# A second transfer on ScalarE's DMA queue: x's half-units 8 to 46 of a scaled addition

## The chip, the cores and the metric

The kernel runs on one core of a Trainium2 chip. A core has five engines with an instruction stream each (TensorE, VectorE or DVE, ScalarE or ACT, GpSimd or POOL, and the sync engine or SP) and 16 DMA engines that move bytes between HBM, the chip's main memory, and SBUF, the core's own memory of 128 partitions. An instruction on SP or ACT issues a transfer; the transfer's share for each DMA engine is then queued there. Engines are tied together by semaphores: a finished instruction or a landed transfer raises one, and others wait for it.

The metric is the device time of one execution in microseconds (us), as the median of several runs.

## The reference

```python
B, S, D = 512, 32, 640
x, fx: (512, 32, 640) bf16, normal * 0.05;  alpha: (1,) bf16
def reference(x, fx, alpha):
    return x + alpha * fx
```

Each of the three large tensors (x, fx and the result) has 10,485,760 elements of two bytes, 20.97 MB. The kernel so reads 41.94 MB, writes 20.97 MB, and does one multiplication and one addition for each element.

## The kernel before

Each large tensor is viewed as 128 rows of 81,920 elements, one row for each partition. A row is cut into 160 half-units of 512 elements, which are 1 KB for each partition and 128 KB for all of them. The whole of x lies in SBUF in one tile, `x_t`, which also takes the result. fx goes through two buffers of 23 half-units (`f_t`, a pool with `bufs=2`).

Four lists say how the work is cut. `X` (line 17) has six loads of x, of 8, 38, 46, 23, 39 and 6 half-units; `F` (line 18) has seven loads of fx, six of 23 half-units and one of 22; `S` (line 19) has three stores, of 64, 64 and 32 half-units. A step of computing, `c j`, belongs to `f j`: on DVE, a `tensor_scalar` (line 96) multiplies the buffer by alpha in place, and a `tensor_tensor` (line 99) adds it to the same columns of `x_t`, in place. So `c 0` works on half-units 0 to 23 and needs x 0, x 1, f 0 and alpha; `c 1` works on 23 to 46 and needs x 1 and f 1; `c 2` needs x 2 and f 2.

The order of all work is the list `PLAN` (lines 22 to 47), written out by hand; nothing is reordered. Its first steps are x 0, x 1, a, f 0, f 1, x 2, c 0, f 2, c 1, f 3, x 3, c 2. The step `a` loads alpha, two bytes, and spreads it to 128 partitions with a `matmul` (line 113) against a row of ones and a copy on DVE (line 115).

Every transfer goes through `transfer` (lines 77 to 82), which issues it on SP. SP works in order. At the start it issues six transfers without waiting: x 0, x 1, alpha, f 0, f 1 and x 2. The transfer f 2 has to wait until `c 0` has read its buffer, f 3 until `c 1` has, and so on. `LATE` (line 48) holds the first store back until f 6 has landed. A last instruction on SP (line 123) waits for everything but the last store.

Of the kernel before, what the change touches and what calls it, by code (L numbers as in the profile page):

```python
# [1 line left out]

# [4 lines left out]

ACT = mybir.ActivationFunctionType
ALU = mybir.AluOpType
F32 = mybir.dt.float32  # L10
BF16 = mybir.dt.bfloat16

K = 512
P = 128


X = [(0, 8), (8, 46), (46, 92), (92, 115), (115, 154), (154, 160)]
F = [(0, 23), (23, 46), (46, 69), (69, 92), (92, 115), (115, 138), (138, 160)]
S = [(0, 64), (64, 128), (128, 160)]
N = 160  # L20

PLAN = """
x 0
x 1
a
f 0
f 1
x 2
c 0
f 2  # L30
c 1
f 3
x 3
c 2
f 4
x 4
c 3
f 5
c 4
f 6  # L40
x 5
c 5
c 6
s 0
s 1
s 2
"""
LATE = {("s", 0): ("f", 6)}


@with_exitstack
def kernel(
    ctx: ExitStack,
    tc: tile.TileContext,
    x: bass.AP,
    fx: bass.AP,
    alpha: bass.AP,
    out: bass.AP,
):
    nc = tc.nc  # L60
    xv = x.flatten_outer_dims().rearrange("(p n) d -> p (n d)", p=P)
    fxv = fx.flatten_outer_dims().rearrange("(p n) d -> p (n d)", p=P)
    ov = out.flatten_outer_dims().rearrange("(p n) d -> p (n d)", p=P)
    assert xv.shape[1] == N * K

    consts = ctx.enter_context(tc.tile_pool(name="consts", bufs=1))
    psum = ctx.enter_context(tc.tile_pool(name="psum", bufs=1, space=bass.MemoryType.PSUM))
    whole = ctx.enter_context(tc.tile_pool(name="whole", bufs=1))
    fs = ctx.enter_context(tc.tile_pool(name="fs", bufs=2))
    ctx.enter_context(tc.manual_schedule())  # L70

    sync = mybir.DependencyInfo(mybir.DependencyClass.Sync, mybir.DependencyReason.DATA)
    xt = whole.tile([P, N * K], x.dtype, name="x_t")
    ft, moved = {}, {}
    done = []

    def transfer(what, out, in_):
        r = nc.sync.dma_start(out=out, in_=in_)  # L78
        if what in LATE:
            tc.add_manual_dep(r.ins, moved[LATE[what]].ins.name, sync, reason="issue late")  # L80
        moved[what] = r
        done.append(r)

    def load_x(i):
        a, b = X[i]
        transfer(("x", i), xt[:, a * K : b * K], xv[:, a * K : b * K])

    def load_f(j):
        a, b = F[j]
        ft[j] = fs.tile([P, max(e - s for s, e in F) * K], fx.dtype, tag="f", name="f_t")  # L90
        transfer(("f", j), ft[j][:, : (b - a) * K], fxv[:, a * K : b * K])

    def compute(j):
        a, b = F[j]
        term, total = ft[j][:, : (b - a) * K], xt[:, a * K : b * K]
        nc.vector.tensor_scalar(  # L96
            out=term, in0=term, scalar1=lanes["a_f"][:], scalar2=None, op0=ALU.mult
        )
        done.append(nc.vector.tensor_tensor(out=total, in0=total, in1=term, op=ALU.add))  # L99

    def store(i):
        a, b = S[i]
        transfer(("s", i), ov[:, a * K : b * K], xt[:, a * K : b * K])

    lanes = {}

    def alpha_to_lanes():
        a_1 = consts.tile([1, 1], alpha.dtype, name="a_1")
        transfer("a", a_1[:], alpha[None, :])
        ones = consts.tile([1, P], alpha.dtype, name="ones")  # L110
        nc.vector.memset(ones[:], 1.0)  # L111
        a_ps = psum.tile([P, 1], F32, name="a_ps")
        done.append(nc.tensor.matmul(a_ps[:], ones[:], a_1[:], start=True, stop=True))  # L113
        lanes["a_f"] = consts.tile([P, 1], F32, name="a_f")
        nc.vector.tensor_copy(out=lanes["a_f"][:], in_=a_ps[:])  # L115

    does = {"x": load_x, "f": load_f, "c": compute, "s": store, "a": alpha_to_lanes}
    for step in PLAN.split("\n"):
        if step:
            what, *of = step.split()  # L120
            does[what](*map(int, of))

    rest = nc.sync.nop(nofuse=True)
    for i in done[:-1]:
        tc.add_manual_dep(rest.ins, i.ins.name, sync, reason="all but the last store")


# [1 line left out]
_INS = ['x', 'fx', 'alpha']  # L129
_OUTS = [((512, 32, 640), 'bfloat16')]  # L130


# [23 lines left out]
```

## Time and profile before

The median of three runs is 151.09 us (151.01 to 151.16). The profile shows one further execution, which took 151.26 us. Its span, from the first instruction to the last, is 149.5 us.

| | |
|---|---|
| profiled execution | 151.26 us |
| its span | 149.5 us |
| DVE busy | 66.7 us, 45% of the span |
| PE and POOL busy | 0.2 us each |
| ScalarE busy | no row in the profile |
| bytes moved by DMA | 62.92 MB, 421 GB/s over the span |
| DMA queue | one, q1, whose packets took 98.2% of the 16 engines' span |
| issue of a transfer on SP | 0.33 to 0.64 us |

In the profile L78 is line 78 of the kernel, "SPq" is SP's sequencer at work on issuing, and "a<-b" says that a is written from b. The time "to landing" of a transfer runs from the start of its issue to its last arrival. A packet is one descriptor's worth of bytes; here each packet is one partition's share of a transfer, so a transfer on 128 partitions has 128 packets of data, eight on each DMA engine. In a table of stretches, a packet is counted in the stretch in which it starts, so that a short stretch can show a DMA share above 1.

### The profile page before, as it was taken

Reading aid. Unit: us, or ns where it says so; the run is one execution under the profiler, and the core shown is the slowest. Engines: PE = TensorE matmul, PEld = TensorE weight load, DVE = VectorE, ACT = ScalarE, POOL = GpSimd, SP = SyncE. Lnnn points to the kernel's source line nnn. Section 1 sums busy time; section 2 is a strip of 40 time slices with the busy share of each in tenths; the row PEclk is TensorE's granted clock in tenths of the full one; section 3 lists DMA queues with packets and bytes.
Section 4 is the critical chain, followed back from the end, with each engine's and each line's share of the span. In section 5 each row is a group of like instructions: output and inputs, shape, how many; then the busy total and the mean of one; then the engine's idle time right before and its main releaser. Section 6 shows DMA issues by size and latency. Waiting matters only on the chain.

```text
span 149.5 us, 93 instructions
## 1 busy us (share of the span) xinstructions
PE 0.2 (0%) x1; PEld 0.1 (0%) x1; DVE 66.7 (45%) x16; POOL 0.2 (0%) x4
## 2 busy tenths in 40 slices
PE   0000000000000000000000000000000000000000
PEld 0000000000000000000000000000000000000000
DVE  0000005999950099999499104999960000000000
POOL 0000000000000000000000000000000000000000
DMA  5998999999979999999998999999996969696994
GB/s 151 463 500 354 448 410 466 435 403 466 542 303 410 466 435 403 429 460 422 443 502 353 417 460 390 458 515 438 403 561 281 561 281 561 281 561 281 456 456 210
DMA packets 2306, 62.92 MB, mean 421 GB/s; under 512 B 258, under 2 KB 258, under 8 KB 386
## 3 DMA queue, kind: packets, MB, share of 16 engines
q1 hardware_dynamic: 2306, 62.92, 98.2%
HBM read 41.94 MB, written 20.97 MB: 421 GB/s over the span
## 4 chain that ended last, share of the span: by engine, by line
DMA 41%; DVE 31%; issue 1%; SPq 1%; DVEq 0%
DMA f_t<-in_fx_dram 41%; DVE x_t L99 20%; DVE f_t L96 11%; SPq L78 1%; DVEq L96 0%
## 5 line engine op out<-in xcount | busy, mean ns | idle before, releaser
L99 DVE TENSOR_TENSOR x_t<-x_t,f_t 128x11776 bf16<-128x11776 bf16 (+1 forms) x7 | 43.8, 6254 | 0.2
L96 DVE TENSOR_SCALAR f_t<-f_t,a_f 128x11776 bf16<-128x11776 bf16 (+1 forms) x7 | 22.9, 3265 | 26.7 <-DMA f_t<-in_fx_dram 26.7
L115 DVE COPY a_f<-a_ps 128x1 f32<-128x1 f32 x1 | 0.2, 159 | 16.2 <-PE a_ps L113 16.2
L111 DVE MEMSET ones<- 1x128 bf16 x1 | 0.2, 165 | 0.8 <-PEq L140 0.8
L113 PE MATMUL a_ps<-a,ones 1*128 1x1 bf16 x1 | 0.2, 158 | 17.0 <-DMA a<-in_alpha_dram 17.0
L140 POOL MEMSET const-bfloat16-1.0<- 128x1 bf16 x1 | 0.1, 101 | 0.0
L140 POOL MEMSET const-uint8-127<- 128x1 uint8 x1 | 0.1, 101 | 0.0
L113 PEld LDWEIGHTS <-ones 1*128 1x128 bf16 x1 | 0.1, 98 | 1.0 <-DVE ones L111 1.0
L140 POOL MEMSET const-float32-0.0<- 128x1 f32 x1 | 0.1, 98 | 0.2 <-issue 0.2
L140 POOL MEMSET const-float32-1.0<- 128x1 f32 x1 | 0.1, 98 | 0.0
## 6 DMA issues: line engine op xcount, KB each, us to landing
f_t<-in_fx_dram SPq DMA_DIRECT2D x6, 2944.0 KB, 19.4
x_t<-in_x_dram SPq DMA_DIRECT2D x1, 5888.0 KB, 41.9
x_t<-in_x_dram SPq DMA_DIRECT2D x1, 4992.0 KB
x_t<-in_x_dram SPq DMA_DIRECT2D x1, 4864.0 KB, 15.9
out_dram<-x_t SPq DMA_DIRECT2D x1, 4096.0 KB, 38.1
x_t<-in_x_dram SPq DMA_DIRECT2D x1, 2944.0 KB, 22.3
f_t<-in_fx_dram SPq DMA_DIRECT2D x1, 2816.0 KB, 15.9
x_t<-in_x_dram SPq DMA_DIRECT2D x1, 1024.0 KB, 4.8
```

Source lines behind the costliest of these rows:

```text
L78: r = nc.sync.dma_start(out=out, in_=in_)
L96: nc.vector.tensor_scalar(out=term, in0=term, scalar1=lanes["a_f"][:], scalar2=None, op0=ALU.mult)
L99: done.append(nc.vector.tensor_tensor(out=total, in0=total, in1=term, op=ALU.add))
L111: nc.vector.memset(ones[:], 1.0)
L113: done.append(nc.tensor.matmul(a_ps[:], ones[:], a_1[:], start=True, stop=True))
L115: nc.vector.tensor_copy(out=lanes["a_f"][:], in_=a_ps[:])
L140: nc = _bacc.Bacc("TRN2", target_bir_lowering=False, num_devices=1)
```

## The change

A table `QUEUE` names the issuing engine of a transfer, and has one entry: the second load of x, half-units 8 to 46, is issued on ScalarE. All other transfers stay on SP, and `PLAN`, the sizes and the computing are the same.

```diff
@@ -45,6 +45,7 @@
 s 1
 s 2
 """
+QUEUE = {("x", 1): lambda nc: nc.scalar}
 LATE = {("s", 0): ("f", 6)}
@@ -75,7 +76,7 @@
     done = []
 
     def transfer(what, out, in_):
-        r = nc.sync.dma_start(out=out, in_=in_)
+        r = QUEUE.get(what, lambda nc: nc.sync)(nc).dma_start(out=out, in_=in_)
         if what in LATE:
```

## The prediction

> **What bounds the kernel now.** I read the page's slices, queue and chain first, then the DMA issues, then a table of stretches, and last the timeline up to 62 us. The page:
>
> ```profile
> DMA  5998999999979999999998999999996969696994
> q1 hardware_dynamic: 2306, 62.92, 98.2%
> HBM read 41.94 MB, written 20.97 MB: 421 GB/s over the span
> DMA 41%; DVE 31%; issue 1%; SPq 1%; DVEq 0%
> x_t<-in_x_dram SPq DMA_DIRECT2D x1, 5888.0 KB, 41.9
> x_t<-in_x_dram SPq DMA_DIRECT2D x1, 4864.0 KB, 15.9
> x_t<-in_x_dram SPq DMA_DIRECT2D x1, 1024.0 KB, 4.8
> ```
>
> The second line decides: the packets of the one queue fill 98.2% of 16 engines' time. The chain names DVE for 31%, but this is one path among several; while DVE works, the engines move bytes too. The last three lines give landings: x 1 (4864 KB) 15.9 us after its issue, x 2 (5888 KB) 41.9 us after. The stretches (length, busy times, clock, DMA share, GB/s):
>
> ```profile
> 1.50:4.00 2.50, 0.00 (x0) 0.00 (x0) 0.00 (x0) 0.00 (x0) 1.00 0.91 275
> 5.00:17.00 12.00, 0.00 (x1) 0.00 (x0) 0.00 (x0) 0.00 (x0) 1.00 0.99 427
> 17.00:24.00 7.00, 0.16 (x1) 0.00 (x0) 0.16 (x1) 0.00 (x0) 1.00 1.00 431
> 45.00:52.00 7.00, 0.00 (x0) 0.00 (x0) 0.00 (x0) 0.00 (x0) 1.00 1.00 431
> 52.00:59.00 7.00, 0.00 (x0) 0.00 (x0) 6.92 (x2) 0.00 (x0) 1.00 1.00 431
> ```
>
> From 5 us on the rate is flat at 427 to 431 GB/s with a share of 1.00, whether DVE works (52 to 59) or not (45 to 52). Only the start is below: 275 GB/s from 1.5 to 4.0 us. One transfer of 23 half-units takes 7.0 us, 0.304 us for each half-unit. The timeline, start and length first:
>
> ```profile
> 0.73 0.86 SPq L78 DMA_DIRECT2D x_t<-in_x_dram  x2
> 1.64 0.33 SPq L78 DMA_DIRECT2D a<-in_alpha_dram  x1
> 2.01 1.03 SPq L78 DMA_DIRECT2D f_t<-in_fx_dram  x2
> 3.08 0.51 SPq L78 DMA_DIRECT2D x_t<-in_x_dram  x1
> 17.00 0.16 PE L113 MATMUL a_ps<-a,ones 1*128 1x1 bf16 x1 [17.00 <-DMA a<-in_alpha_dram]
> 24.19 3.29 DVE L96 TENSOR_SCALAR f_t<-f_t,a_f 128x11776 bf16<-128x11776 bf16 x1 [6.84 <-DMA f_t<-in_fx_dram]
> 27.51 6.29 DVE L99 TENSOR_TENSOR x_t<-x_t,f_t 128x11776 bf16<-128x11776 bf16 x1
> 33.83 9.85 SPq L78 DMA_DIRECT2D f_t<-in_fx_dram  x2
> 52.05 3.29 DVE L96 TENSOR_SCALAR f_t<-f_t,a_f 128x11776 bf16<-128x11776 bf16 x1 [8.71 <-DMA f_t<-in_fx_dram]
> ```
>
> SP has issued 138 half-units by 3.6 us, and they keep the engines busy until x 2 lands at 3.08 + 41.9 = 45.0 us. The next transfer, f 2, is issued at 33.83 us, when c 0 is done, 11 us before the engines would run dry; it lands just before 52.05 us, one transfer time after x 2. So the time is the start, plus all bytes at a fixed rate, plus the end, as long as SP's issues stay ahead.
>
> **The change, part by part.** The profiled execution took 151.26 us for a span of 149.5 us, so 1.76 us lie outside the span; it stands 0.17 us above the median of 151.09, and I subtract that from a sum on the span.
>
> Removed from SP: one issue. The two issues of x took 0.86 us together, so about 0.45 us; alpha, f 0, f 1 and x 2 are issued that much earlier, x 2 at 2.6 us. Worth nothing: their bytes wait behind x 0 and x 1 (f 0 is issued at 2.01 us and lands at 24.1), and SP then idles until 33.83 us.
>
> Added on ScalarE: one issue of about 0.43 us. ScalarE has no row in the profile, so nothing queues behind it. By the trace's records it leaves the starting barrier at 0.67 us, as SP does, so it can issue x 1 at about 0.75 us beside x 0, instead of at 1.17 us behind it. x 0's first packet starts at 1.74 us, 1.01 us after its issue began; x 1's first can then start at about 1.76 us. Cost: nothing, since x 0 fills the engines from 1.74 us anyway.
>
> Moved: the order in which the engines serve 69 half-units (x 0, x 1, f 0) and perhaps parts of f 1. Their sum is unchanged, so x 2, or whatever of the first six ends last, still lands at 45.0 us if the rate holds. If the engines alternate packet by packet, eight packets of 8 KB meet eight of 38 KB on each engine; x 0 and x 1 end together near 17 us and f 0 lands at 24.1 us as before. If they share by bytes, f 0 ends after 62 half-units, at 24.1 - 7 x 0.304 = 22.0 us, and x 1 after 76, at 24.1 + 7 x 0.304 = 26.2 us. The multiplication of c 0 then runs 22.1 to 25.4 us and the addition starts at 26.3 instead of 27.51 us. Either way c 0 is done by 33.8 us, f 2 is in the queue before 45.0 us, and the 1.2 us gained on DVE are spent waiting for f 2.
>
> SP's last waits (line 123) include x 1, wherever it was issued; it has landed a hundred microseconds earlier. At the end x 1 leaves no trace.
>
> The unknown costs are two, and both lie where the engines are the bound. First, the start. The 128 packets of x 0 took 10.3 us more in sum than their usual 309 ns each, 0.65 us for each engine, nearly all in the first and second packet; the stretch says the same: 2.5 us at 275 instead of 431 GB/s is 0.90 us, of which 0.24 us lie before the first packet. A second queue could fill these gaps, for a gain of at most 0.65 us, or open as slowly itself while the first one waits, for a loss of at most 0.65 us. I take 0: the first packet waits for its first bytes from HBM, and so would the second queue's. Second, the switching. Before, no two queues compete, so no row prices it. Nearest is a change of the stream: x 1's first packet after x 0 took 1473 ns instead of 1439, and the longest of the first store's after the loads 2451 instead of 2418, that is 33 or 34 ns. With 16 switches for each engine (in and out of eight packets) this is 16 x 0.034 = 0.54 us; nothing at the other end, since most packets follow the one before them with no gap and no excess. I take 0.1 us, near the lower end, since nearly all packets at a change of transfer (f 2 after x 2, x 3 after f 3) show at most 11 ns of excess.
>
> Sum: 151.26 - 0.17 - 0 + 0.1 = 151.2 us.
>
> A rule of the Trainium skill bears on this. "DMA: Bandwidth & Descriptors", section "Issuing engines are not separate DMA queues", says that transfers issued from several engines run on the same 16 DMA engines and interleave, and that issuing from several only saves the sequencer's time. By it the change is worth the 0.45 us of SP's issue at the most, and by the trace nothing, since no one waits for that issue. Its section "Queues, rings and completion order" has each engine take turns between the queues, packet by packet; by that x 1 is not left behind and the starvation below can't happen. No row before shows two queues, so I leave that rival a small chance.
>
> **The rivals.** A, the forecast: the same bytes at the same rate, 151.2 us, within about 0.3 us either way. For it: the flat 431 GB/s and the idle SP and ScalarE.
>
> B, a fuller start: the second queue's packets move during the slow opening of the first. For it: the 275 GB/s, and that x 1 is issued 0.45 us sooner. Against it: x 0 alone has eight packets queued on each engine, so it isn't a lack of work that holds the first packet. It pays between 0.3 and 0.65 us, 150.4 to 150.8; 150.6 us.
>
> C, dearer sharing: while x 1 and SP's transfers compete, until about 17 to 26 us, each change of queue costs some tens of nanoseconds on each engine, or the second queue opens as slowly as the first. For it: the 33 ns at a change of stream, the slow opening. Against it: nearly no excess inside a stream of transfers. Nothing hides it, since the engines never run dry later: it goes into the end one for one. 0.54 us for the switches gives 151.6, with a second opening of 0.65 us 152.3; I say 151.9 us. It decides from 0.3 us on, which is 19 ns for each of 16 switches.
>
> D, starvation: SP's queue is served first and x 1 lands last, at 45.0 us. The addition of c 0 then runs 45.1 to 51.3 us, f 2 is issued at 51.4, needs 1.0 us to its first packet where the engines ran dry at about 44.6, so 7.8 us are lost; f 3 waits for c 1, issued at 51.3 + 3.3 + 6.3 = 60.9 us, with first packets at 61.9, where f 2's end is at 59.4, 2.5 us more. About 161 us. It decides only when x 1 lands after 35 us: c 1 must end by 51.0 us for f 3 to follow f 2 at 52.0, which is c 0 by 41.4 and its addition's start by 35.1.
>
> E, no effect at all because x 1 still goes through the same queue: 151.1 us. The profile after has one queue row then.
>
> **How the numbers follow.** A 0.42, B 0.22, C 0.30, D 0.04, E 0.02. What a measurement of this kernel can tell from no change is about 0.2%, 0.3 us. Of A, 0.36 lies within it, 0.02 is faster and 0.04 slower; E is within. So faster 0.02 + 0.22 = 0.24, same 0.36 + 0.02 = 0.38, slower 0.04 + 0.30 + 0.04 = 0.38. The range goes from 150.5, which leaves out the best of B (some 0.07), to 152.4, above C's upper price; above it lie D and some 0.07 of C for a sharing that costs more than any row shows. The forecast's own range is 150.8 to 151.5 us.
>
> **What would show it.** A second queue row with x 1's 4864 KB, 4.98 MB, and q1 with the remaining 57.94 MB; together still about 98%. x 0 lands later than 4.8 us after its issue, which proves the sharing. The test of the rate is when x 2 lands: 45.0 us in A, 44.4 to 44.7 in B, 45.5 to 46.2 in C; c 2's multiplication, now at 52.05 us, must follow by the same amount, and so must the end. A wait of DVE for x_t before c 0's addition beyond 35 us would show D. The prediction is wrong if sharing changes the rate itself, in the sharing stretch or after it, or if x 1's queue opens much later than 1.8 us.

## The result, and the profile after

The change makes the kernel slower by 0.35%: 151.70 us (151.63 to 151.77) against 151.14 us (151.01 to 151.20) for the kernel before, six runs each (for the kernel before, the three above and three more); the ratio is 1.0035, with a 95% interval of 1.0025 to 1.0045. A later comparison, in which the kernel before took 151.35 us, gave 1.0026 (1.0017 to 1.0035). The profiled execution took 151.69 us with a span of 149.9 us, 0.43 us more than the one before on both counts.

From the page of the changed kernel: the DMA slices, the two queues, and the landings of the first three loads of x (kilobytes, us from issue to landing).

```profile
DMA  6999999999989999999999999999896969696993
q1 hardware_dynamic: 2162, 57.93, 90.2%
q10 hardware_dynamic: 144, 4.98, 7.8%
x_t<-in_x_dram SPq DMA_DIRECT2D x1, 5888.0 KB, 42.8
x_t<-in_x_dram ACTq DMA_DIRECT2D x1, 4864.0 KB, 16.9
x_t<-in_x_dram SPq DMA_DIRECT2D x1, 1024.0 KB, 16.8
```

The change did what it says: x 1's 4.98 MB are now on a queue of their own, and the two together fill 98.0% of the engines' span, as one did before. The last line proves the sharing: x 0 landed 4.8 us after its issue before, and now takes 16.8, because x 1's packets stand between its own.

The same stretches as before (length, busy times, clock, DMA share, GB/s), then the timeline.

```profile
1.50:4.00 2.50, 0.00 (x0) 0.00 (x0) 0.00 (x0) 0.00 (x0) 1.00 1.00 311
5.00:17.00 12.00, 0.08 (x1) 0.00 (x0) 0.00 (x0) 0.00 (x0) 1.00 0.97 417
17.00:24.00 7.00, 0.16 (x1) 0.00 (x0) 0.16 (x1) 0.00 (x0) 1.00 1.01 434
45.00:52.00 7.00, 0.00 (x0) 0.00 (x0) 0.00 (x0) 0.00 (x0) 1.00 1.00 431
```

```profile
0.73 0.38 SPq L79 DMA_DIRECT2D x_t<-in_x_dram  x1
0.73 0.40 ACTq L79 DMA_DIRECT2D x_t<-in_x_dram  x1
2.62 0.51 SPq L79 DMA_DIRECT2D x_t<-in_x_dram  x1
24.61 3.29 DVE L97 TENSOR_SCALAR f_t<-f_t,a_f 128x11776 bf16<-128x11776 bf16 x1 [7.34 <-DMA f_t<-in_fx_dram]
27.93 6.29 DVE L100 TENSOR_TENSOR x_t<-x_t,f_t 128x11776 bf16<-128x11776 bf16 x1
34.26 9.85 SPq L79 DMA_DIRECT2D f_t<-in_fx_dram  x2
52.48 3.29 DVE L97 TENSOR_SCALAR f_t<-f_t,a_f 128x11776 bf16<-128x11776 bf16 x1 [8.72 <-DMA f_t<-in_fx_dram]
```

The loss is complete by the first multiplication: c 0 starts at 24.61 instead of 24.19 us, 0.42 us late, c 2 at 52.48 instead of 52.05, 0.43 us late, and the span ends 0.43 us late. From 45 us on the rate is the same 431 GB/s. So something in the first 24 us cost 0.42 us, and nothing gave it back or added to it.

The stretches don't show what: more bytes start between 1.5 and 4 us (311 against 275 GB/s), fewer until 17. The 16 engines have to be taken apart. A landing is complete when the last of 16 engines reports; the trace has all 16 times. For x 2, the last of the six transfers issued at the start, they are, in us:

```
            earliest   mean   latest   span   span minus latest
before        44.61   44.84   45.02  149.48       104.46
after         44.47   44.89   45.45  149.91       104.46
```

The earliest engine is faster than before, the mean is 0.06 us later (before rounding), and the latest 0.43 us later. The end follows the latest engine to within 0.01 us. The lag stays once it is there: between the earliest and the latest engine lie 0.98 us at f 0's landing and 0.98 us at f 2's, in the kernel before 0.42 and 0.41. The packets of single engines (the records of the trace, length in ns; "S" is SP's queue, "A" ScalarE's, then KB) show where the late ones lost it. The records don't name the engine; a packet is put to the engine whose packet before it ends as it starts.

```
before, one near the middle S8 1174  S8 309   S8 309   S8 309   S8 319 ...  S38 1439 S38 1439 ...
after, earliest engine      S8 361   A38 1832 S8 309   A38 1439 S8 309   A38 1439 ...
after, a late engine        S8 787   A38 1458 S8 320   A38 1942 S8 309   A38 1439 ...
after, next to latest       S8 1594  A38 1448 S8 309   A38 1439 S8 309   A38 1439 ...
after, latest engine        S8 1531  A38 1448 S8 309   A38 1439 S8 309   A38 1439 ...
```

The engines take turns strictly, one packet from each queue, and after the opening the packets have their usual length, 309 or 1439 ns (one took 37 ns more, the others less than that). The excess lies in the first two to four packets of an engine. Its largest sum on one engine, over x 0 and x 1, is 1.29 us after and 0.95 us before; the mean over the 16 engines is 0.73 us after and 0.66 us before.

The section "Queues, rings and completion order" of the Trainium skill's page "DMA: Bandwidth & Descriptors" has each engine take turns between the queues packet by packet, and gives a packet as typically about 9 to 17 descriptors. The trace agrees on the turns and not on their length: here an engine turned after every single descriptor, of 8 or 38 KB.

### The profile page after: what moved, and what is told of

It reads as the page before. It is cut to its first block, busy times and chain, and to the rows that moved or that the text cites. A ratio compares the mean times of both kernels' runs of the same rounds, so it can differ in the third digit from the quotient of the medians.

```text
span 149.9 us, 93 instructions
## 1 busy us (share of the span) xinstructions
PE 0.2 (0%) x1; PEld 0.1 (0%) x1; DVE 66.7 (44%) x16; POOL 0.2 (0%) x4
## 3 DMA queue, kind: packets, MB, share of 16 engines
q10 hardware_dynamic: 144, 4.98, 7.8%
## 4 chain that ended last, share of the span: by engine, by line
DMA 41%; DVE 31%; issue 1%; SPq 0%; DVEq 0%
DMA f_t<-in_fx_dram 41%; DVE x_t L100 20%; DVE f_t L97 11%; SPq L79 0%; DVEq L97 0%
## 6 DMA issues: line engine op xcount, KB each, us to landing
f_t<-in_fx_dram SPq DMA_DIRECT2D x1, 2816.0 KB, 15.9
x_t<-in_x_dram SPq DMA_DIRECT2D x1, 1024.0 KB, 16.8
```

## The experiments

The runs took place on three chips, on which the kernel before has medians of 151.18, 151.37 and 151.35 us (25, 33 and 33 runs), so a time is compared only with the kernel before of the same comparison. The kernel before has one trace only, from the first measurement, and traces from different chips are compared with the same caution. The theories: O, two queues that open together on idle engines open less evenly; P, large packets served in the opening do, whichever queue they come from; Q, ScalarE's queue is slower in itself; S, each change of queue costs.

### ScalarE's queue alone in the opening

```diff
-QUEUE = {("x", 1): lambda nc: nc.scalar}
-LATE = {("s", 0): ("f", 6)}
+QUEUE = {("x", 0): lambda nc: nc.scalar, ("x", 1): lambda nc: nc.scalar}
+LATE = {("s", 0): ("f", 6), "a": ("x", 0)}
```

> x 0 and x 1 are both issued on ScalarE, and SP holds alpha and all that follows until x 0 has landed (about 5.5 us), so only one queue opens on the idle engines, and it is ScalarE's. Theory O (two queues that open together on idle engines open less evenly; the slowest engine sets the end): 151.1 us as before, x 0 and x 1 end on the slowest engine at about 16.7 us, though x 1 shares the engines with f 0 for most of its way. Rival Q (ScalarE's queue is slower in itself, to open or for each packet): 151.6 us or more. Rival S (each change of queue costs some 30 ns while both hold packets): with 8 packets of x 1 between f 0's, 151.5 to 151.7 us.

Measured: 151.13 us against 151.18, ratio 0.9997 (0.9989 to 1.0006). From the page and the timeline of this run:

```profile
x_t<-in_x_dram ACTq DMA_DIRECT2D x1, 4864.0 KB, 21.2
x_t<-in_x_dram ACTq DMA_DIRECT2D x1, 1024.0 KB, 4.8
24.16 3.29 DVE L97 TENSOR_SCALAR f_t<-f_t,a_f 128x11776 bf16<-128x11776 bf16 x1 [12.99 <-DMA f_t<-in_fx_dram]
52.01 3.29 DVE L97 TENSOR_SCALAR f_t<-f_t,a_f 128x11776 bf16<-128x11776 bf16 x1 [8.71 <-DMA f_t<-in_fx_dram]
```

x 0 lands 4.8 us after its issue on ScalarE's queue, exactly as on SP's; x 1 shares with f 0 (21.2 instead of 15.9 us), so the expectation that it ends at 16.7 us on the slowest engine was wrong, but c 0 and c 2 start where they did before. Q is out. S predicted at least 151.5 us and is out as well.

### x 1 on ScalarE after the opening

```diff
-LATE = {("s", 0): ("f", 6)}
+LATE = {("s", 0): ("f", 6), ("x", 1): ("x", 0)}
```

> As the changed kernel, but x 1 on ScalarE is held back until x 0 has landed (about 5.5 us), while SP's queue holds alpha, f 0, f 1 and x 2; the two queues then share engines that are running. x 1 lands near 24 to 26 us, early enough for c 0 (it may land as late as 35). Theory O: 151.1 us, x 2 lands at about 45.0 us after the span's start. Rival S: 16 changes of queue for each engine as in the changed kernel, so 151.6 to 151.7 us, with x 2 or x 1 later by 0.4 to 0.5 us.

Measured: 151.17 us against 151.18, ratio 1.0000 (0.9992 to 1.0009). From its timeline:

```profile
5.53 0.37 ACTq L79 DMA_DIRECT2D x_t<-in_x_dram  x1
18.35 3.29 DVE L97 TENSOR_SCALAR f_t<-f_t,a_f 128x11776 bf16<-128x11776 bf16 x1 [12.69 <-DMA f_t<-in_fx_dram]
28.00 6.29 DVE L100 TENSOR_TENSOR x_t<-x_t,f_t 128x11776 bf16<-128x11776 bf16 x1 [6.36 <-DMA x_t<-in_x_dram]
51.99 3.29 DVE L97 TENSOR_SCALAR f_t<-f_t,a_f 128x11776 bf16<-128x11776 bf16 x1 [8.17 <-DMA f_t<-in_fx_dram]
```

The whole transfer of the change, on the same queue and in competition with SP's, costs nothing once the engines run. All 128 packets of x 1 took 1439 to 1441 ns, between packets of 23 KB from the other queue. A new wait appears, 6.36 us of DVE for x 1, and it is harmless as the prediction's bound of 35 us said: x 1 lands at 27.9 us, later than the 24 to 26 that I expected, and c 2 still waits for f 2. So the loss needs the opening.

### The roles exchanged

```diff
-QUEUE = {("x", 1): lambda nc: nc.scalar}
+QUEUE = {("x", 0): lambda nc: nc.scalar}
```

> x 0 (packets of 8 KB) on ScalarE, x 1 (38 KB) and all others on SP, nothing held back: two queues open together, with the roles exchanged. Theory O: 151.6 us, spread of the 16 engines at f 0's landing near 1.0 us instead of 0.42. Rival Q: ScalarE's queue now carries 1 MB instead of 5 MB, so the loss shrinks to 0.1 us or so. Rival S: 16 changes of queue again, 151.6 us, which can't be told from O by the time, but by the packets, which would exceed their usual length all along.

Measured: 151.68 us against 151.18 (five runs), ratio 1.0033 (1.0021 to 1.0046); the spread of f 0's landing was 0.61 us, and not near the 1.0 that O expected. From its timeline, c 2's multiplication:

```profile
52.35 3.29 DVE L97 TENSOR_SCALAR f_t<-f_t,a_f 128x11776 bf16<-128x11776 bf16 x1 [8.72 <-DMA f_t<-in_fx_dram]
```

The loss is that of the change, though ScalarE now carries only 1 MB, which Q had put at 0.1 us. The packets of x 0 are 309 ns without exception, all 128 of them, where S wanted excess all along; the whole excess is in x 1's first packets, which took up to 2556 ns instead of 1439.

### One queue, the large transfer first

```diff
-X = [(0, 8), (8, 46), (46, 92), (92, 115), (115, 154), (154, 160)]
+X = [(0, 38), (38, 46), (46, 92), (92, 115), (115, 154), (154, 160)]
```

(The edit is to the kernel before; all transfers are on SP.)

> The kernel before with x 0 and x 1 exchanged in size: the first transfer has 38 half-units, the second 8, all on SP. Theory O: one queue opens alone, 151.1 us, spread at f 0's landing about 0.42 us. Rival P (the opening is uneven because of the large packets that are in the engines when they start, not because of the second queue): 151.5 to 151.7 us, spread near 1.0 us.

Measured: 151.54 us against 151.18, ratio 1.0025 (1.0015 to 1.0035), spread at f 0's landing 0.68 us. From its page and timeline:

```profile
q1 hardware_dynamic: 2306, 62.92, 98.1%
24.46 3.29 DVE L96 TENSOR_SCALAR f_t<-f_t,a_f 128x11776 bf16<-128x11776 bf16 x1 [7.05 <-DMA f_t<-in_fx_dram]
52.32 3.29 DVE L96 TENSOR_SCALAR f_t<-f_t,a_f 128x11776 bf16<-128x11776 bf16 x1 [8.72 <-DMA f_t<-in_fx_dram]
```

This run has one queue and most of the loss: c 0 is 0.27 us late, c 2 too. My theory O falls as I had put it; a second queue isn't needed. P's time came about, its spread of near 1.0 us did not. What the changed kernel, the exchange and this run have in common is that every engine meets a packet of 38 KB among its first two.

### Two queues with small packets in the opening

```diff
-X = [(0, 8), (8, 46), (46, 92), (92, 115), (115, 154), (154, 160)]
+X = [(0, 8), (8, 16), (46, 92), (92, 115), (115, 154), (154, 160), (16, 46)]
 x 0
 x 1
+x 6
 a
```

(x 1, now half-units 8 to 16, is on ScalarE; x 6 is on SP.)

> Two queues open together as in the changed kernel, but what ScalarE issues is only half-units 8 to 16, in packets of 8 KB like x 0's; half-units 16 to 46 follow on SP behind x 0. Theory P (the opening is uneven where large packets are served in the first 2 us or so of the DMA engines' work, whichever queue they come from): 151.1 to 151.2 us, slowest engine's landing of x 2 at 45.0 us after the span's start. Rival O (two queues that open together are the cause, whatever the packets): 151.5 to 151.7 us, 45.3 us or later.

Measured: 151.43 us against 151.37, ratio 1.0002 (0.9993 to 1.0011). Two queues that open together cost nothing that this comparison shows when both bring packets of 8 KB. The latest landing of x 2, 45.23 us, lies between P's 45.0 and O's 45.3, and decides nothing, since the kernel before has no trace on this chip. It was repeated on one chip with the changed kernel:

> The changed kernel once more, on the same chip as the next three. All theories: 0.35% over the kernel before, about 0.5 us.

> Half-units 8 to 16 on ScalarE, 16 to 46 on SP, once more beside the changed kernel. Theory P (large packets in the opening): as the kernel before, within 0.1%, and 0.25% or more below the changed kernel. Rival O (two queues that open together): as the changed kernel.

The changed kernel took 151.71 us against 151.35 (1.0026, 1.0017 to 1.0035), this one 151.49 (1.0009, 1.0000 to 1.0018). Rival O, which wanted them equal, is out as the whole cause. P wanted 0.25% or more between the two, and 0.15% was measured: small packets take away 0.22 of the 0.36 us, and whether the other 0.14 us is noise or the price of the second queue can't be told, since the interval goes from 0 to 0.18%.

### All of x 1 on ScalarE, in two pieces

```diff
-X = [(0, 8), (8, 46), (46, 92), (92, 115), (115, 154), (154, 160)]
-QUEUE = {("x", 1): lambda nc: nc.scalar}
+X = [(0, 8), (8, 16), (46, 92), (92, 115), (115, 154), (154, 160), (16, 46)]
+QUEUE = {("x", 1): lambda nc: nc.scalar, ("x", 6): lambda nc: nc.scalar}
 x 0
 x 1
+x 6
 a
```

> All of the changed transfer's bytes on ScalarE, but as two transfers, half-units 8 to 16 and then 16 to 46: its first eight packets on each engine have 8 KB, and its packets of 30 KB come after about 6 us, when SP's queue has come to alpha and f 0. Theory P: as the kernel before, within 0.1%. Rival O, and rival S (sharing costs for as long as it lasts): 0.3% or more over it.

Measured: 151.44 us against 151.35, ratio 1.0006 (0.9997 to 1.0015). The same bytes are on the same queue as in the change, issued as early, and by the medians three quarters of the loss are gone (0.27 of 0.36 us); by the interval, what is left may be anything up to 0.15%. What differs is that ScalarE's first packets have 8 KB and that its large ones, now 30 KB in a transfer of their own, start only at 7.5 us; all 128 of these took 1138 ns. c 2's multiplications on this chip, the changed kernel's first:

```profile
52.68 3.29 DVE L97 TENSOR_SCALAR f_t<-f_t,a_f 128x11776 bf16<-128x11776 bf16 x1 [8.72 <-DMA f_t<-in_fx_dram]
```

```profile
52.23 3.29 DVE L98 TENSOR_SCALAR f_t<-f_t,a_f 128x11776 bf16<-128x11776 bf16 x1 [8.72 <-DMA f_t<-in_fx_dram]
```

They stand 0.45 us apart in these two executions; the medians differ by 0.27 us.

### How the loss depends on the size

Four kernels with one queue differ from the kernel before only in the cut between x 0 and x 1: `(0, 2), (2, 46)`, `(0, 4), (4, 46)`, `(0, 16), (16, 46)` and `(0, 23), (23, 46)`.

> The kernel before with x 0 cut to 2 half-units and x 1 enlarged to 44; all on SP. x 0's eight packets of 2 KB take under 0.1 us each, so x 1's packets of 44 KB come within the first 2 us of the engines' work. Theory P: 151.3 to 151.6 us. Rival O (only a second queue hurts) is out for a single queue, by the run with the large transfer first; if x 0's size only matters by the very first packet on each engine: 151.1 us or a little less.

> The kernel before with x 0 of 4 half-units and x 1 of 42, all on SP: first packets of 4 KB, of which eight last about 1.2 us. Theory P: between a gain of 0.1 us (smaller packets open more evenly) and a loss of 0.2 us (x 1's large packets come too early).

> The kernel before with x 0 of 16 half-units and x 1 of 30, all on SP: first packets of 16 KB. Theory P with a smooth dependence on the size: between 151.1 and 151.55 us, about 151.25. With a threshold near 38 KB: 151.1 us.

> The kernel before with x 0 and x 1 of 23 half-units each, all on SP: first packets of 23 KB, between the 16 KB that cost nothing and the 38 KB that cost 0.25%. Theory P, smooth between: 0.1% over the kernel before, 151.25 us where that takes 151.1; with a step between 16 and 23 KB: 0.25%; between 23 and 38: 0.

| first packets, then the second transfer's | ratio to the kernel before | 95% interval |
|---|---|---|
| 2 KB, then 44 KB | 1.0012 | 1.0003 to 1.0020 |
| 4 KB, then 42 KB | 1.0008 | 0.9999 to 1.0016 |
| 16 KB, then 30 KB | 1.0001 | 0.9992 to 1.0010 |
| 23 KB, then 23 KB | 1.0007 | 0.9998 to 1.0016 |
| 38 KB, then 8 KB | 1.0025 | 1.0015 to 1.0035 |

Each ratio is to the kernel before on the same chip; the rows of 2, 4 and 16 KB come from one chip, those of 23 and 38 KB from two others. Two rows are clear of no change, the smallest and the largest. The smallest fits P: packets of 2 KB are soon over (84 ns each at their usual length), and 44 KB packets come into the opening, from 2.62 us on, the longest of them 2420 ns instead of 1665. Between 4 and 23 KB the differences are within the measurement, so these rows don't show how the loss grows with the size. None of these kernels is faster than the kernel before.

### All executions together

Landing of x 2 on the 16 engines, and the span, in us, for each profiled execution; the time of the profiled execution and the median stand beside them.

| kernel | earliest | mean | latest | span | span minus latest | profiled, median |
|---|---|---|---|---|---|---|
| before | 44.61 | 44.84 | 45.02 | 149.48 | 104.46 | 151.26, 151.14 |
| after | 44.47 | 44.89 | 45.45 | 149.91 | 104.46 | 151.69, 151.70 |
| ScalarE alone first | 44.37 | 44.57 | 44.98 | 149.47 | 104.50 | 151.26, 151.13 |
| x 1 late | 44.44 | 44.70 | 44.96 | 149.43 | 104.47 | 151.21, 151.17 |
| exchanged | 44.71 | 44.96 | 45.32 | 149.81 | 104.48 | 151.59, 151.68 |
| 38 KB first | 44.63 | 44.90 | 45.28 | 149.76 | 104.48 | 151.54, 151.54 |
| small, two queues | 44.58 | 44.91 | 45.23 | 149.69 | 104.46 | 151.48, 151.43 |
| after, again | 44.62 | 45.04 | 45.66 | 150.13 | 104.48 | 151.91, 151.71 |
| small, again | 44.72 | 44.95 | 45.20 | 149.72 | 104.52 | 151.51, 151.49 |
| x 1 in two pieces | 44.65 | 44.89 | 45.21 | 149.67 | 104.46 | 151.46, 151.44 |
| 2 KB first | 44.61 | 44.86 | 45.36 | 149.82 | 104.45 | 151.60, 151.59 |
| 4 KB first | 44.53 | 44.85 | 45.34 | 149.92 | 104.59 | 151.72, 151.47 |
| 16 KB first | 44.64 | 44.91 | 45.47 | 149.95 | 104.48 | 151.73, 151.39 |
| 23 KB first | 44.50 | 44.83 | 45.15 | 149.64 | 104.49 | 151.42, 151.43 |

The span is the latest engine's landing of x 2 plus 104.45 to 104.59 us in every kernel. What is decided by 45 us is decided for good, and by the slowest of 16 engines: with ScalarE alone first, the mean engine was 0.27 us earlier than in the kernel before, the latest 0.04 us and the span 0.01 us. The row for 16 KB warns that a single execution's opening scatters: its trace is 0.34 us above its median. The verdicts therefore rest on the medians, and the traces only say where the time goes.

## Why the prediction was right, and where its terms were wrong

The range of 150.5 to 152.4 us holds the measured 151.70, but the forecast itself, 151.2 within about 0.3 us, is short by 0.5 us, and the case that came about is nearest to rival C, at 151.6 to 152.3 us. The range reached that far only for C's two prices, and neither of C's reasons is what the runs show; that it holds the result is in this part luck.

- *SP's issue, worth nothing*: right. x 2 is issued at 2.62 instead of 3.08 us, and no load of x or fx lands sooner.
- *ScalarE's issue, 0.43 us from about 0.75 us*: right, 0.40 us at 0.73.
- *The order of the first 69 half-units*: right, for engines that alternate packet by packet: x 0 lands at 17.5 and x 1 at 17.7 us, where I had said near 17.
- *The start, "I take 0"*: this term failed. I argued that the second queue's first packets wait as the first one's do, which holds for the mean engine (x 2's mean landing moved by 0.06 us), and overlooked that the end hangs on the slowest of 16 engines. There it cost 0.43 us, inside the 0.65 us that I had given as the bound. The bound came from a mean, too; one engine before had already lost 0.95 us. That a first packet waits for its first bytes from HBM, the reason I gave, is shown by no run.
- *The switching, 0.1 us between 0 and 0.54*: no cost was found. C's first reason is refuted by the run with x 1 held back, and its price of 0.54 us fits the loss by chance. Its second reason, that the second queue opens as slowly as the first, had the right place but not the cause, since one queue with large packets first loses 0.36 us as well, and ScalarE's queue alone opens with no loss.
- *B*: the earliest engine did gain (44.47 against 44.61 us), which is worth nothing while the latest loses. *D*: no starvation; the queues take turns. *E*: the second queue is there.
- *The test named*: x 2's landing and c 2's multiplication moving by the same amount as the end was the right place to look, 0.43 us in all three. Landing at 45.45 us is just below the 45.5 named for C.

The rule of the Trainium skill ("DMA: Bandwidth & Descriptors", "Issuing engines are not separate DMA queues"), that issuing from several engines only saves sequencer time, agrees with this trace as far as a gain goes: x 2 was issued 0.46 us sooner, and nothing ended sooner. The loss of 0.35% is known from the runs alone.

So the term that was mis-sized is the start: put at 0, it measured 0.43 us on the slowest engine. That large packets in the opening cost time, whichever queue brings them, is shown by the run with one queue; that they are most of the loss of the change is shown by the two kernels with small first packets. What stays open is whether a part of some 0.1 us belongs to the second queue, and why packets of 38 KB open less evenly than packets of 8 KB. The traces show which packets are long, not what they wait for.

## What to carry to other kernels

In this kernel the DMA engines are the bound nearly from the first microsecond to the last. A second issuing queue bought nothing in it, and what the engines were served in their first three microseconds, from 1.7 to 4.6 us, decided the end: each engine has its own eight of a transfer's 128 packets, and the slowest of 16 set every landing after it. So in a kernel of this kind read the 16 arrivals of one landing, not only its last, and read a change at the start from the first transfer that all others queue behind. If a second queue is wanted for other reasons, small packets (8 KB here) at its opening, or a start once the engines run, are worth a trial; both left the median within 0.1% of the kernel before.

## What the runs showed that was not expected

- One queue alone loses 0.25% when its first packets have 38 KB instead of 8 KB, with the same bytes in the same order of columns.
- Two queues share an engine packet by packet at no cost to the packets: in the run with x 1 held back, 128 packets of 38 KB between packets of 23 KB took 1439 to 1441 ns, as on one queue.
- Where the large packet is an engine's first, nearly all of the excess is in it, and a few engines have far more of it than the others: with 38 KB first on one queue, four engines took 2434 to 2487 ns for that packet, the other twelve 1752 to 2132.
- A packet in the opening can take up to 2556 ns instead of 1439 (the exchanged roles), and such an excess also hits a third or fourth packet (1942 ns in the changed kernel) after others near full speed.
